# An expert mixture with a long convolution on one core: no GpSimd arithmetic in the head, tokens normalised inside the first expert, the first expert by halves

## The chip, the cores and the metric

The kernel runs on one core of a Trainium2 chip. TensorE (PE in the profile, with PEld for its weight loads), VectorE (DVE), ScalarE (ACT), GpSimd (POOL) and SyncE (SP) each take their own instructions in a fixed order and wait for each other by semaphores. DMA queues move data between HBM and the on-chip memory SBUF; matmul results land in PSUM. The metric is the device time of one execution in microseconds (us). "The span" is the stretch from the first to the last instruction in the profile.

## What is computed

Both branches read the same normalised tokens: a gated convolution (two depthwise convolutions over 2048 positions) and a mixture of 8 experts with 2 chosen for each token.

```python
def _A_ref(q, k, v, shift_k, ssm_k, ssm_D):          # B, S, D = 1, 2048, 512
    ...
    for t in range(ks):                                # ks = 4
        k_shift = k_shift + k_pad[:, t:t + S, :] * shift_k[:, ks - 1 - t][None, None, :]
    kv = k_shift * v
    ...                                                # y = long causal convolution of kv with ssm_k, by FFT
    y = y + kv * ssm_D[None, None, :]
    return q * y

def _B_ref(x, w_gate, w1, w2):                         # D, F, E = 512, 1792, 8
    ...
    logits = xf @ w_gate
    topk_idx = jnp.argsort(-logits, axis=-1)[:, :K]    # K = 2
    topk_val = jnp.take_along_axis(logits, topk_idx, axis=-1)
    gates = _softmax(topk_val, axis=-1)
    for e in range(E):
        mask = (topk_idx == e)
        w = (gates * mask).sum(-1, keepdims=True)
        h = _silu(xf @ w1[e]) @ w2[e]
        out = out + w * h
    ...

x = A_q
xn = _layernorm(x, axis=-1)
return x + _A_ref(xn, A_k, A_v, A_shift_k, A_ssm_k, A_ssm_D) + _B_ref(xn, B_w_gate, B_w1, B_w2)
```

## The kernel before

**Stages.** A head (`load_x`, `logits`, `routing`) finds for each token its two experts and for each expert the list of its tokens. Then eight experts run one after the other (`expert`), the fullest first, with 576 places for the first. The convolution's work is cut into small pieces which `fill` hands out between the matmuls of the experts. Three pieces of it, `conv_k` for the groups (0,3), (1,0) and (1,1), are recorded in `routing` instead, behind `prep(0)`; `conv_k` turns eight columns of the filter (`ptk`, L641), multiplies them by the transform's edge matrix (`ps`, L606) and stores them in `zk_d`.

**The token columns.** The 2048 tokens lie as 16 columns of 128 tokens by 512 numbers, in four tiles `x` of four columns, in a pool of their own. `bn_stats` gives mean and variance, `rstds` the scale `rstd` and the shift `nmr`. In `norm` GpSimd normalises twelve columns (L310) and ScalarE four (L307); `store_xn` writes them to `xn_d` in DRAM, from where the other experts gather their tokens.

**The first expert's tokens.** A one-hot table and matmuls (`ptab`) give the list of token numbers (`gix`). `gathers` then has GpSimd issue six indirect DMAs, each of which fetches 96 rows of the raw input into a block `xg`. The blocks are normalised by scales gathered through a second table matmul, three on ScalarE and three on VectorE (L847, L849). `turn` transposes them on TensorE into `ptm`, and since matmuls take numbers of reduced precision here, each operand is split in two: ScalarE rounds to `xh` ("high"), VectorE subtracts to `xl` ("low"). Weights are split the same way into `wh` and `wl`: `weights` loads 512 KB slices `wraw`, three buffers in turn.

**An expert.** `mm6` multiplies high by high, low by high and high by low. An expert has 14 hidden tiles (numbered 0 to 13 here): each is 24 matmuls into one of two PSUM tiles `ps`; ScalarE applies silu twice (`h` rounded, `ht` full), VectorE subtracts to the low part (L912). Two hidden tiles come from one weight slice. In the first expert `weights` has GpSimd make the low part `wl` of slices 1 to 5 (`lo_eng`), VectorE that of the others. Behind each hidden tile `fill` also does a step of `slots`, which makes the token lists of the other experts: VectorE writes a table (`tabA`, `tabB`, `tabR`), TensorE multiplies it (`ptab`, 128x216), VectorE adds the result to `tb`.

**What sets the order.** A scheduler sorts the recorded instructions of each engine with a time model of its own; a call `after(late, early, reason)` holds one instruction behind another without a wait. So the second half of the convolution's filter is held behind the gathers by a one-element GpSimd write:

```python
            if pair:
                self.after(nc.gpsimd.memset(t[:1, c, :1], 0.0), self.gather, "the first expert's tokens come first")
            nc.sync.dma_start(t[:, c, :], io["A_ssm_k"][dc * P:(dc + 1) * P, :])
```

Each engine then keeps that order: an instruction which waits holds back all behind it.

## Time and profile before

| what | value |
|---|---|
| time, median of 3 runs | 893.86 us (892.17 to 895.03) |
| the profiled execution's own time | 892.98 us |
| its span | 891.1 us |
| TensorE busy | 840.8 us (94%) |
| VectorE busy | 599.9 us (67%) |
| ScalarE busy | 501.0 us (56%) |
| GpSimd busy | 234.1 us (26%) |
| mean granted TensorE clock | 0.975 of full speed |

Rows of a timeline have the start in us from the span's start, the duration in us, the engine, the line, the operation, what it writes <- what it reads with shapes, and the count; in brackets stands how long the engine had been idle just before and who ended that. Rows of a table by stage have the stage, its length, then for each engine the busy us and the number of instructions, then the granted clock, the share of the DMA engines and GB/s.

### The profile page before, as it was taken

What the parts mean: (1) busy time and instruction counts of PE and PEld (TensorE: products, weight loads), DVE (VectorE), ACT (ScalarE), POOL (GpSimd) and SP (SyncE); (2) the same over time, 40 slices, a digit from 0 to 9 for tenths busy, and PEclk for the clock granted to TensorE, in tenths of its full rate; (3) what the DMA queues carried; (4) which work ended last, traced back from release to release, by engine and by line L of the source; (5) the groups of instructions that cost most, each with busy time, mean ns of one, the idle gap of its engine ahead of it and who ended that gap; (6) DMA issues with size and microseconds to landing.
All of it is one profiled execution on the core that took longest, in us unless ns stands there. A gap on an engine that the chain in (4) does not pass through costs nothing. (4 is left out here: it accounts for less than half of the span.)

```text
span 891.1 us, 13814 instructions
## 1 busy us (share of the span) xinstructions
PE 840.8 (94%) x5040; PEld 734.6 (82%) x5040; DVE 599.9 (67%) x841; ACT 501.0 (56%) x786; POOL 234.1 (26%) x202
## 2 busy tenths in 40 slices
PE   9807999999999998999999999999999989999996
PEld 7506899888999888999999988888888767777885
DVE  6893674679866765567766677658766649965421
ACT  4625542435533455666876668657875659654520
POOL 0090304046330440304310050103201123444222
PEclk9957999999999999999999999999999999999999
DMA  7595754999977676665965666557655499968972
GB/s 304 174 328 199 274 177 135 278 234 287 243 199 208 180 205 210 206 183 171 237 197 167 194 214 215 180 177 232 228 171 174 134 251 297 282 197 286 263 209 71
DMA packets 146497, 190.97 MB, mean 214 GB/s; under 512 B 12673, under 2 KB 106235, under 8 KB 144956
## 3 DMA queue, kind: packets, MB, share of 16 engines
q1 hardware_dynamic: 130348, 147.29, 54.4%
q0 software_dynamic: 16080, 42.78, 16.6%
q8 instruction: 41, 0.67, 0.3%
q14 instruction: 28, 0.23, 0.1%
HBM read 143.88 MB, written 50.63 MB: 218 GB/s over the span
## 5 line engine op out<-in xcount | busy, mean ns | idle before, releaser
L869 DVE TENSOR_TENSOR wl<-wraw,wh 128x1024 fp32r<-128x1024 f32 (+1 forms) x111 | 135.0, 1216 | 110.1 <-ACT wh L866 99.9
L866 ACT ACTIVATE wh<-wraw 128x1024 fp32r<-128x1024 f32 (+1 forms) x116 | 119.3, 1029 | 149.7 <-PE ps L884 109.9
L884 PE MATMUL ps<-xh,wh 128*128 128x512 f32 (+4 forms) x672 | 183.8, 328 | 5.6 <-ACT ht L911 2.9
L884 PE MATMUL ps<-xl,wh 128*128 128x512 f32 (+4 forms) x672 | 182.8, 326 | 0.0
L884 PE MATMUL ps<-xh,wl 128*128 128x512 f32 (+4 forms) x672 | 182.0, 325 | 0.0
L884 PE MATMUL ps<-h,wh 128*128 128x288 f32 (+3 forms) x896 | 154.3, 291 | 0.0
L884 PEld LDWEIGHTS ps<-h,wh 128*128 128x128 f32 x896 | 129.0, 189 | 5.6 <-issue 4.5
L884 PEld LDWEIGHTS ps<-xh,wh 128*128 128x128 f32 x672 | 113.7, 190 | 22.1 <-ACT ht L911 5.1
L884 PEld LDWEIGHTS ps<-xl,wh 128*128 128x128 f32 x672 | 114.2, 190 | 8.7
L884 PEld LDWEIGHTS ps<-xh,wl 128*128 128x128 f32 x672 | 113.8, 190 | 9.0
L912 DVE TENSOR_TENSOR h<-ht,h 128x512 fp32r<-128x512 f32 (+4 forms) x112 | 79.7, 717 | 44.3 <-ACT ht L911 44.1
L910 ACT ACTIVATE h<-ps 128x512 fp32r<-128x512 f32 (+4 forms) x112 | 67.8, 605 | 61.7 <-PE ps L884 58.1
L884 PE MATMUL ps<-h,wl 128*128 128x288 f32 (+3 forms) x448 | 95.5, 291 | 0.0
L957 PE MATMUL py<-wl,h 128*128 128x512 f32 x224 | 87.6, 391 | 0.0
L958 PE MATMUL py<-wh,h 128*128 128x512 f32 x224 | 87.5, 391 | 0.0
L956 PE MATMUL py<-wh,h 128*128 128x512 f32 x224 | 87.1, 392 | 0.0
L938 POOL DMA_INDIRECT acc_d<-acc,ids x36 | 54.0, 1499 | 120.7 <-DVE acc L936 114.0
L884 PEld LDWEIGHTS ps<-h,wl 128*128 128x128 f32 x448 | 71.7, 189 | 1.9 <-issue 1.5
L923 POOL DMA_INDIRECT acc<-acc_d,gix x36 | 46.8, 1300 | 99.1 <-PE ptx L828 64.3
L911 ACT ACTIVATE ht<-ps 128x512 f32<-128x512 f32 (+4 forms) x112 | 67.9, 609 | 0.0
L809 POOL DMA_INDIRECT xg<-xn_d,gix x34 | 41.4, 1218 | 82.2 <-PE ptx L828 40.6
L738 DVE TENSOR_TENSOR ka<-pu,ka 128x512 f32<-128x512 f32 x32 | 22.1, 691 | 50.5 <-ACT ka L733 43.2
(241 smaller groups left out, 1288.3 us busy)
## 6 DMA issues: line engine op xcount, KB each, us to landing
wraw<-in_B_w_dram SPq DMA_DIRECT2D x84, 512.0 KB, 4.6
wraw<-in_B_w_dram SPq DMA_DIRECT2D x32, 448.0 KB, 4.6
zk_d<-ev SPq DMA_DIRECT2D x16, 512.0 KB, 6.7
zv_d<-ev SPq DMA_DIRECT2D x16, 512.0 KB, 6.3
mid<-in_c_mid_dram POOLq DMA_DIRECT2D x16, 512.0 KB, 5.4
z<-zk_d SPq DMA_DIRECT2D x32, 256.0 KB, 3.0
z<-zv_d SPq DMA_DIRECT2D x32, 256.0 KB, 3.1
zi_d<-zo SPq DMA_DIRECT2D x32, 256.0 KB, 3.4
```

Source lines behind the costliest of these rows:

```text
L809: self.gather = nc.gpsimd.indirect_dma_start(out=t[:sb], out_offset=None, in_=self.xn_d[:, :] if r else self.io["A_q"].rearrange("o s d -> ...
L866: w = nc.scalar.activation(hi, raw, AF.Copy)
L869: t = (lo_eng or nc.vector).tensor_sub(lo, raw, hi)
L884: nc.tensor.matmul(ps[:, u, :n], w, x[:, u, :], start=first and w is wh and k == 0, stop=last and w is wl)
L910: nc.scalar.activation(h, ps[:, :nu, :n], AF.Silu)
L911: acts.append(nc.scalar.activation(t, ps[:, :nu, :n], AF.Silu))
L912: self.hid = nc.vector.tensor_sub(l, t, h)
L923: nc.gpsimd.indirect_dma_start(out=acc[:sb], out_offset=None, in_=sum_d[:, :], in_offset=bass.IndirectOffsetOnAxis(ap=self.gix[:sb, c0 + b ...
L938: st = nc.gpsimd.indirect_dma_start(out=sum_d[:, :], out_offset=bass.IndirectOffsetOnAxis(ap=self.ids[:sb, c0 + b:c0 + b + 1], axis=0), in ...
L956: nc.tensor.matmul(o, a, wh[:, f, :], start=ff == 0, stop=False)
L957: nc.tensor.matmul(o, a, wl[:, f, :], start=False, stop=False)
L958: nc.tensor.matmul(o, l, wh[:, f, :], start=False, stop=ff == FC - 1)
```

## The change

Four things change. **GpSimd computes nothing** any more in the head and the first expert: the low parts of weight slices 1 to 5 go to VectorE, the token columns to VectorE and ScalarE (eight each), and the one-element writes are gone, so that the filter's second half is loaded as soon as its queue allows. **The token columns** lie in eight tiles of two columns, in a pool `h2` under the names `h6` to `h13`: these are the places of the last eight hidden tiles. The first two tiles are normalised behind the first expert's tokens, tile i (2 to 7) behind hidden tile i-2, and each is stored at once; hidden tile 6+i is written into the place of token tile i. **The first expert begins by halves**: blocks 0 to 2 are normalised, transposed and split before blocks 3 to 5, and hidden tiles 0 and 1 are accumulated for the first half of the tokens, then for the second; VectorE normalises all six blocks. **The gates** are a tanh, from the table that also holds silu, in place of an exponential and a reciprocal. With this the order is written anew: the one-hot table in four parts, the gathers ahead of the three convolution groups and these ahead of the tokens, VectorE taking every second eviction of the last two groups, and the rest of the routing's arithmetic behind the last low part `xlo`.

```diff
     def load_x(...)
-            t = ep.tile([P, 4, D], F32, tag="x", name="x", bufs=4)
+            t = self.h2.tile([P, 2, D], F32, tag="h%d" % (FC - NI // 2 + i), name="x")
...
     def norm(self):
-                if j == 3:
-                    self.after(nc.scalar.activation(x[:, j, :], x[:, j, :], AF.Identity, bias=bi, scale=sc),
-                               self.parted, "the first expert comes first")
-                else:
-                    t = nc.gpsimd.tensor_scalar(x[:, j, :], x[:, j, :], sc, bi, op0=ALU.mult, op1=ALU.add)
-                    self.pool_norms.append(t)
...
+            v = nc.vector.tensor_scalar(self.x[2 * i], self.x[2 * i], sc, bi, op0=ALU.mult, op1=ALU.add)
+            sc, bi = self.rstd[:, 2 * i + 1:2 * i + 2], self.nmr[:, 2 * i + 1:2 * i + 2]
+            a = nc.scalar.activation(self.x[2 * i + 1], self.x[2 * i + 1], AF.Identity, bias=bi, scale=sc)
+            if i < 2:
+                self.after(v, self.xlo, "the first expert comes first")
+                self.after(a, self.xhi, "the first expert comes first")
+            else:
+                self.norms.append((v, a))
+            self.xs.append(nc.sync.dma_start(xnv[:, 2 * i:2 * i + 2, :], self.xt[i]))
...
     def routing(self, bp, sp, cp):
-        self.onehot(A0, f0, 2)
         self.columns(B0, q0)
...
+        self.rtid = self.onehot(A0, f0, 4, t)
...
+        t = nc.scalar.activation(self.warm, self.warm, AF.Silu)
+        self.after(t, self.rooted, "the square root comes first")
+        self.after(nc.scalar.activation(gt, gt, AF.Tanh, scale=0.5), t, "one table serves both")
...
+        self.gathers(0)
+        for pair, q8 in ((0, 3), (1, 0), (1, 1)):
+            for _ in self.conv_k(cp, pair, q8, pair == 1):
+                pass
         self.prep(0)
-        for pair, q8 in ((0, 3), (1, 0), (1, 1)):
-            for _ in self.conv_k(cp, pair, q8):
-                pass
-        self.store_xn()
...
-        self.after(V.tensor_mul(w8, ro, b1(rt["cap"])), self.indexed, "the routing comes first")
+        self.after(V.tensor_mul(w8, ro, b1(rt["cap"])), self.xlo, "the first expert comes first")
...
     def pairs(...)
-            for t, ev in zip(ps, evs):
-                nc.scalar.activation(ev[:, r, :], t, AF.Copy)
+            for k, (t, ev) in enumerate(zip(ps, evs)):
+                if shared and k:
+                    nc.vector.tensor_copy(ev[:, r, :], t)
+                else:
+                    nc.scalar.activation(ev[:, r, :], t, AF.Copy)
...
     def load_k(self, cp, pair):
-            if pair:
-                self.after(nc.gpsimd.memset(t[:1, c, :1], 0.0), self.gather, "the first expert's tokens come first")
...
     def prep(self, r):
-        for b in range(0 if r else NBLK[r]):
-            t, (sc, bi) = self.xg[b][:sb], (a[:sb, b:b + 1] for a in self.sc0)
-            if b % 2:
-                self.normed = nc.scalar.activation(t, t, AF.Identity, bias=bi, scale=sc)
-            else:
+        for u in range(2):
+            for b in range(3 * u, 3 * u + 3):
+                t, (sc, bi) = self.xg[b][:sb], (a[:sb, b:b + 1] for a in self.sc0)
                 nc.vector.tensor_scalar(t, t, sc, bi, op0=ALU.mult, op1=ALU.add)
+            self.turn(0, [u])
+            if u == 0:
+                self.half = self.xhi
+        self.norm()
...
     def weights(...)
-        t = (lo_eng or nc.vector).tensor_sub(lo, raw, hi)
-        if self.nw == 1:
+        t = nc.vector.tensor_sub(lo, raw, hi)
+        if self.nw < 3:
             self.after(t, self.scaled, "the first expert's tokens come first")
...
     def expert(self, hp, r, fill):
+            if r == 0 and s == 0:
+                ahead = [self.pmm.tile([P, 2, D], F32, tag="mm", name="ps") for _ in range(2)]
+                for u in range(nu):
+                    for f in range(2):
+                        for dc in range(DC):
+                            self.mm6(ahead[f], nu, n, wh[:, dc, f * P:(f + 1) * P], wl[:, dc, f * P:(f + 1) * P],
+                                     self.xh[dc], self.xl[dc], dc == 0, dc == DC - 1, u)
...
+                hl2 = (hp if ff < FC - NI // 2 else self.h2).tile([P, 2, nu, n], F32R, tag="h%d" % ff, name="h")
...
+                if self.norms:
+                    for late, early in zip(self.norms.pop(0), (self.hid, acts[-1])):
+                        self.after(late, early, "the first expert comes first")
...
```

How this moves the instructions stands below at three places; the rows are those of an engine's own order, with line, operation, what it writes <- what it reads and the shape. Numbers behind a name tell buffers apart.

**VectorE, around the first expert's tokens.** Names: `xg` a gathered block, `xl` the tokens' low part, `wl` a weight slice's low part, `ev` an evicted spectrum, `wk`, `o`, `ef`, `blk` arithmetic of the routing. Before:

```order
L474 TENSOR_TENSOR pos_488<-pos_488,iso_798 128x128
L511 TENSOR_SCALAR ef_849<-ef_849 1x32
L849 TENSOR_SCALAR xg_596<-xg_596,sc00_592,sc01_593 96x512
L479 TENSOR_TENSOR wk_814<-oh_448,pos_488 128x256
L512 CAST blk_85<-ef_849 1x32
L480 TENSOR_REDUCE o_805<-wk_814 128x32
```

Now:

```order
L845 TENSOR_SCALAR xg_619<-xg_619,sc00_607,sc01_608 96x512
L832 TENSOR_TENSOR xl_722<-ptx_726,xh_718 128x288
L832 TENSOR_TENSOR xl_723<-ptx_732,xh_719 128x288
L832 TENSOR_TENSOR xl_724<-ptx_738,xh_720 128x288
L832 TENSOR_TENSOR xl_725<-ptx_744,xh_721 128x288
L864 TENSOR_TENSOR wl_1063<-wraw_1060,wh_1062 128x1024
L845 TENSOR_SCALAR xg_621<-xg_621,sc00_607,sc01_608 96x512
L832 TENSOR_TENSOR xl_722<-ptx_753,xh_718 128x288
L832 TENSOR_TENSOR xl_723<-ptx_759,xh_719 128x288
L832 TENSOR_TENSOR xl_724<-ptx_765,xh_720 128x288
L832 TENSOR_TENSOR xl_725<-ptx_771,xh_721 128x288
L304 TENSOR_SCALAR x_106<-x_106,rstd_126,nmr_127 128x512
```

The routing's arithmetic stood between the blocks; all of it now stands behind the last low part and two token columns (`x`), and the third weight slice stands between the two halves. Ahead of these rows VectorE has, in this order: the first two weight slices, two evictions `ev`, the first three blocks, an eviction, a block, an eviction.

**VectorE, up to the first table of the other experts' lists.** Names: `h` a hidden tile's low part, `cc` the last of the routing's arithmetic, `tabA`, `tabB`, `tabR` the table. Before:

```order
L500 TENSOR_TENSOR cc_812<-cc_812,tq_811 128x32
L835 TENSOR_TENSOR xl_637<-ptm_638,xh_636 128x576
L835 TENSOR_TENSOR xl_648<-ptm_649,xh_647 128x576
L912 TENSOR_TENSOR h_908<-ht_907,h_908 128x576
L521 TENSOR_TENSOR tabA_913<-rc_116,f6_813 128x512
L527 TENSOR_TENSOR tabB_914<-rc_116,cc_812 128x288
```

Now:

```order
L496 TENSOR_TENSOR cc_836<-cc_836,tq_835 128x32
L912 TENSOR_TENSOR h_956<-ht_955,h_956 128x576
L304 TENSOR_SCALAR x_110<-x_110,rstd_126,nmr_127 128x512
L517 TENSOR_TENSOR tabA_961<-rc_123,f6_837 128x512
L526 TENSOR_TENSOR tabB_962<-rc_123,cc_836 128x288
L912 TENSOR_TENSOR h_967<-ht_966,h_967 128x576
L304 TENSOR_SCALAR x_112<-x_112,rstd_126,nmr_127 128x512
L534 TENSOR_TENSOR tabR_963<-tabB_962,tid2_870 128x4x72
```

The last of the arithmetic stood ahead of the tokens' last low parts; it now stands behind them, and a token column follows each hidden tile.

**TensorE, hidden tile 3 and the first table.** Names: `ps_998` and `ps_1021` are the PSUM tiles of hidden tile 3, `ptab` the table's product. Before:

```order
L884 MATMUL ps_998<-xh_636,wl_960 128x288 x2
L884 MATMUL ps_998<-xh_647,wh_959 128x288 x2
L884 MATMUL ps_998<-xl_648,wh_959 128x288 x2
L884 MATMUL ps_998<-xh_647,wl_960 128x288
L537 MATMUL ptab_948<-tabR_915,tabA_913 128x216 x4
```

Now:

```order
L876 MATMUL ps_1021<-xh_719,wh_982 128x288 x2
L876 MATMUL ps_1021<-xl_723,wh_982 128x288 x2
L876 MATMUL ps_1021<-xh_719,wl_983 128x288 x2
L536 MATMUL ptab_971<-tabR_963,tabA_961 128x216 x4
L876 MATMUL ps_1021<-xh_720,wh_982 128x288 x2
```

The table's product stood one matmul before the end of tile 3; it now stands in its middle, behind 12 of its 24 matmuls.

## What was predicted

> **What bounds the kernel now.** First the page: whose engine is the span. Then the busy times by stage, to see where that engine rests.
>
> ```profile
> span 891.1 us, 13814 instructions
> PE 840.8 (94%) x5040; PEld 734.6 (82%) x5040; DVE 599.9 (67%) x841; ACT 501.0 (56%) x786; POOL 234.1 (26%) x202
> ...
> 40.00:50.00 10.00, 3.02 (x34) 2.84 (x32) 6.39 (x42) 5.44 (x8) 6.04 (x6) 0.70 1.09 339
> 50.00:60.00 10.00, 0.00 (x0) 0.00 (x0) 10.00 (x6) 3.39 (x4) 10.00 (x11) 0.50 1.10 311
> 60.00:70.00 10.00, 2.00 (x9) 1.43 (x10) 9.83 (x24) 0.00 (x0) 7.04 (x10) 0.50 0.63 239
> ...
> 160.00:891.00 731.00, 714.25 (x4196) 624.02 (x4194) 495.46 (x586) 427.79 (x664) 190.06 (x153) 0.99 0.72 211
> ```
>
> TensorE (PE) works 94% of the span and 714 of the last 731 us, so the kernel is a queue of matmuls, and what an edit is worth is how much earlier that queue runs freely. It rests between 43 and 75 us: 5 of 30 us busy, at half the clock. So the next view is that stretch in order of time, engine by engine; each row has start, duration and engine.
>
> ```profile
> 39.98 1.52 PE L537 MATMUL ptab<-tabR,tabA 128*96 128x6 f32 x16
> 65.64 0.90 PE L828 MATMUL ptm<-ident,xg 96*128 96x96 f32 x4 [22.12 <-DVE xg L849]
> 75.00 0.85 PE L884 MATMUL ps<-xh,wh 128*128 128x288 f32 x2 [0.57 <-DVE xl L835]
> 83.86 1.99 PE L606 MATMUL ps<-kt,ev 64*128 64x512 f32 x8
> 91.51 0.63 PE L884 MATMUL ps<-xh,wh 128*128 128x288 f32 x2 [1.89 <-ACT ht L911]
> 95.53 0.42 PE L884 MATMUL ps<-xh,wh 128*128 128x288 f32 x2
> 95.79 0.43 PE L884 MATMUL ps<-xl,wh 128*128 128x288 f32 x2
> 99.97 0.30 PE L884 MATMUL ps<-xh,wh 128*128 128x288 f32 x1
> ...
> 51.13 14.02 DVE L511 TENSOR_SCALAR ef<-ef 1x32 f32<-1x32 f32 x1
> 65.06 0.53 DVE L849 TENSOR_SCALAR xg<-xg,sc,sc 96x512 f32<-96x512 f32 x1
> ...
> 52.23 4.63 POOL L869 TENSOR_TENSOR wl<-wraw,wh 128x1024 fp32r<-128x1024 f32 x2
> 56.86 9.72 POOL L310 TENSOR_SCALAR x<-x,rstd,nmr 128x512 f32<-128x512 f32 x12
> 66.55 0.48 POOL L628 TENSOR_TENSOR ks<-ks,dv 128x1 f32<-128x1 f32 x2
> ```
>
> TensorE waits 22.12 us for the first normalised token block, and that block waits behind one VectorE (DVE) instruction on 32 numbers that takes 14.02 us. GpSimd (POOL) computes without a pause from 52.23 to 66.6, so I read the 14 us as VectorE shut out by GpSimd. A second pair, forty microseconds later, says the same: a 0.46 us instruction (its neighbour at 99.51, below) takes 2.64 and ends as GpSimd's does.
>
> ```profile
> 93.57 2.56 POOL L869 TENSOR_TENSOR wl<-wraw,wh 128x1024 fp32r<-128x1024 f32 x1 [14.41 <-ACT wh L866]
> ...
> 93.80 2.64 DVE L535 TENSOR_TENSOR tabR<-tabB,tid 128x288 fp32r<-128x288 f32 x1
> ...
> 99.51 0.46 DVE L535 TENSOR_TENSOR tabR<-tabB,tid 128x288 fp32r<-128x288 f32 x1
> ```
>
> The Trainium skill, page "SBUF — State Buffer", section "Who interferes with whom", has it as a lock: a GpSimd instruction and certain VectorE ones share one port pair, and the later one stands still for the whole of the other. The trace agrees (14.02 and 2.64 us).
>
> After 75 us two costs remain: the last two convolution groups sit inside the first expert (83.86 on), and tile 2 of the expert starts cold at 91.51. Tile 4 starts at 99.97; from there on TensorE is full. **My mark is the start of tile 4**: before it everything is moved, behind it nothing but VectorE's load.
>
> **The change part by part.**
>
> *Step 1, the indices: +1.1 us.* The gathers now start when?
>
> ```profile
> 42.44 1.10 POOL L809 DMA_INDIRECT xg<-in_A_q_dram,gix  x1 [20.11 <-DVE tb L544]
> 48.75 2.72 POOL L809 DMA_INDIRECT xg<-in_A_q_dram,gix  x1 [0.30 <-issue]
> ...
> 44.11 1.28 ACT L449 ACT_TABLE_LOAD   x1
> ...
> DMA to landing us min/median/max: 6.0/6.8/8.8
> ```
>
> The one-hot table is cut in four and its matmuls follow piece by piece, which would save most of their 1.52 us. But on TensorE the products of group (0,3) now stand between the pieces, and they wait for ScalarE (ACT), whose table load of 1.28 us has moved ahead of those evictions. So the last piece ends near 43.0 in place of 41.5; VectorE's copy into SBUF drops out (0.2 us), the gate's logistic needs no exponential table and no wait. Bounds: 0 if the evictions lead anyway, +1.5 if all of the load shows. I take a start at 43.5.
>
> *Step 2, the landing: gather 3 at 52.8, gather 6 at 58.6.* The six issues come (48.75 - 42.44)/5 = 1.26 us apart. Gather 3: 43.5 + 2 × 1.26 + 6.8 (median). Gather 6: 43.5 + 5 × 1.26 + 8.8 (the longest, because the weight loads and spectrum stores are in flight now too; the DMA share was 1.09 to 1.10 before). Bounds for gather 6: 55.8 with 6.0, and 58.6 plus the extra issue time of rival 2. ssm_k's second half (2 MB) leaves this stretch for that of 20 to 30 us, whose DMA share is 0.02, and costs nothing there:
>
> ```profile
> 20.00:30.00 10.00, 8.49 (x52) 5.12 (x50) 9.33 (x29) 5.29 (x11) 0.19 (x1) 1.00 0.02 7
> ```
>
> *Step 3, convolution groups (1,0), (1,1): hidden, -7.6 us on the path.* They took TensorE from 83.86 to 91.51 with ScalarE's evictions. Now they stand between the gathers and the token transposes, in the 22 us hole. VectorE takes every second eviction. They pass if done by about 54, when half the tokens are there; without that cover each group costs about 4 us.
>
> *Step 4, tokens to VectorE's last low part: 61.4.* GpSimd computes nothing, so the 14.02 goes. VectorE does in this order (durations as start-to-start pitches of its rows): gather 3's block done 53.3; two evictions and two blocks to 55.7; four low parts of half width, 0.37 each (half of 0.75), 57.2; the third weight split, 1.13, 58.3; gather 6's block 59.1; transposes, ScalarE's high parts and four low parts, 61.4. The halves let TensorE do 12 matmuls of tile 0 in that time, no more. Bounds 58 (gather 6 at the median) to 66.
>
> *Step 5, VectorE's small arithmetic lands on the path: to 75.8.* Routing's second part, 56 small instructions that before lay beside the waiting, now stands behind the low parts, and the first slot table behind it.
>
> ```profile
> 45.73 0.24 DVE L456 TENSOR_TENSOR w<-ro,rt 128x64 f32<-128x64 f32 x1
> 49.07 1.20 DVE L869 TENSOR_TENSOR wl<-wraw,wh 128x1024 fp32r<-128x1024 f32 x1
> 50.20 0.27 DVE L472 TENSOR_TENSOR col<-col,cb 128x128 f32<-128x128 f32 x1
> 65.52 0.41 DVE L479 TENSOR_TENSOR wk<-oh,pos 128x256 f32<-128x256 f32 x1
> 72.31 0.75 DVE L835 TENSOR_TENSOR xl<-ptm,xh 128x576 fp32r<-128x576 f32 x1
> 72.98 0.18 DVE L500 TENSOR_TENSOR cc<-cc,tq 128x32 f32<-128x32 f32 x1
> 97.75 0.76 DVE L912 TENSOR_TENSOR h<-ht,h 128x576 fp32r<-128x576 f32 x1 [0.57 <-ACT ht L911]
> 98.42 0.68 DVE L521 TENSOR_TENSOR tabA<-rc,f 128x512 fp32r<-128x512 f32 x1
> 100.62 0.38 DVE L572 COPY tb<-ptab 128x216 f32<-128x216 f32 x1
> ```
>
> First part: 45.73 to 51.13 plus 0.16 is 5.56, less the split (50.20 - 49.07 = 1.13) and about 0.7 of six small ones that go or come earlier: 3.75. Second part: 65.52 to 73.10 is 7.58, less two token blocks (0.46 each) and two low parts (0.67 each): 5.3. With the first two token columns (0.46 each, as a block) 9.95: VectorE is at 71.35. Then, until the first slot table is written: two hidden tiles (98.42 - 97.75 = 0.67 each), two token columns, and table parts (100.62 - 98.42 = 2.2): 4.45. **Table ready at 75.8.**
>
> TensorE reaches that table's matmul in the middle of tile 3: behind the last low part 26 matmuls of tiles 0 and 1, 24 of tile 2, 12 of tile 3, at (95.79 - 95.53)/2 = 0.13 us: 62 × 0.134 = 8.3, so at 69.7. It waits 6.1 us, with tiles 3 to 13 queued behind. Before, VectorE had been idle there, and the table never waited:
>
> ```profile
> 91.49 0.76 DVE L912 TENSOR_TENSOR h<-ht,h 128x576 fp32r<-128x576 f32 x1 [15.58 <-ACT ht L911]
> ```
>
> The clock falls: rows 91.51 to 95.53 hold 18 matmuls in 4.02 us in place of 2.41, so 1.6 is lost. Tile 4 starts at 75.8 + 0.44 (table) + 12 × 0.134 + 1.6 = **79.45**, against 99.97: **-20.5 us**.
>
> *Step 6, later in the first expert: 0.* Five weight splits move from GpSimd (2.56 above) to VectorE (1.13), and of the sixteen token columns VectorE and ScalarE now take eight each. VectorE per two tiles: 2 × 0.67 + 2.2 + 0.36 + 1.13 + 2 × 0.46 = 5.95, TensorE 48 × 0.134 + 0.44 = 6.9. It keeps up by 0.9; if that is off by 1 us, three such pairs cost 3. Each of tiles 6 to 13 waits for its tokens' store: the column comes after tile i-2 and the place is wanted at tile i+6, eight tiles or 26 us later; the four stores before took 6.9 us to land:
>
> ```profile
> xn_d<-x SPq DMA_DIRECT2D x4, 1024.0 KB, 6.9
> ```
>
> Sum: 891.1 - 20.5 = 870.6 span. The profiled execution took 892.98 us (1.9 around the span), the median of three is 893.86, so the profile is 0.9 below that; my time is 870.6 + 1.9 = 872.5.
>
> **The rivals.**
>
> *1, no stall at the table.* If VectorE's small instructions run much faster than their rows, or TensorE is so slow and cold until then that it comes no earlier than the table, nothing waits: tile 4 at 61.4 + 74 × 0.134 + 0.44 = 71.8, gain 28.2, **864.8 us**. Against it: 14.4 us of VectorE stand against 8.3 of TensorE, in a fixed order.
>
> *2, gathers late.* The sixth gather's issue took 2.72 us, the five others about 0.92, and VectorE's 1.20 us split ran in it (49.07). Now two splits and two evictions run during gathers 4 to 6: (2.72 - 0.92) for two of them is 3.6, and the low parts end near 65: **876 us** (874 to 880). The same page of the Trainium skill, in "A bandwidth-pool intuition that's wrong", says GpSimd cannot write a gather's descriptors while VectorE holds the pair; by it the moved work, token blocks above all, hits the gathers. The 2.72 fits, and no run here yet shows which instruction does it.
>
> *3, the 14 us stay*, since GpSimd's gathers and not its arithmetic shut VectorE out: 872.5 + 14 = **886**. Against: the row ends with the arithmetic, 15 us after the last issue.
>
> *4, slower: the places.* The stores of pairs 2 to 7 stand on SyncE's queue behind a register load that waits for VectorE and behind weight loads. It decides when column, store and landing together exceed 26 us; six tiles then each wait, and one tile's time (3.2) each is 19 us, so a little over that is **897**. Against: 0.5 + 6.9 + the few us of queue.
>
> **How the numbers follow.** Forecast 0.54 (872), rival 1 0.13, rival 2 0.25, rival 3 0.04, rival 4 0.04. 864 to 880 holds the forecast with the last low part at 58 to 66 and a cold stall or not, and rivals 1 and 2. Under 0.3% (2.7 us) this kernel's measurement cannot tell a change from none. Faster 0.95, same 0.02, slower 0.03 (rival 4, split).
>
> **What would show it.** Step 1: first gather near 43.5. Step 2: VectorE's last token block near 58.6 and no 14 us instruction. Step 3: no spectrum products after 56. Step 5: TensorE idle about 6 us before the first 128x216 table matmul, released by VectorE, and a half clock behind it; without that idle time rival 1 is right. Rival 2: issues above 2 us. Step 6: no wait of the activation on a store, TensorE full from tile 4 on. The forecast is wrong if the gathers land outside 55 to 61, or if TensorE stalls again at a later table.

## The result

The changed kernel takes 872.7 us (median of four runs, 872.59 to 874.25) against 894.44 us before (four runs, 892.17 to 895.2): the ratio is 0.9765, 95% interval 0.9743 to 0.9787. A second set of runs, in a later sitting, gave 872.66 us (six runs, 870.28 to 875.4) and 0.9786 (0.9757 to 0.9814). Forecast were 872.5 us and a range of 864 to 880.

The page of the changed kernel and its busy times by stage (stage, length, busy us and instructions of TensorE, its weight loads, VectorE, ScalarE and GpSimd, then the granted clock, the DMA share and GB/s):

```profile
span 872.5 us, 13843 instructions
PE 843.4 (97%) x5040; PEld 735.1 (84%) x5040; DVE 597.2 (68%) x864; ACT 499.3 (57%) x786; POOL 209.8 (24%) x183
...
50.00:60.00 10.00, 7.75 (x32) 4.88 (x33) 6.88 (x13) 5.58 (x11) 0.44 (x1) 0.57 1.03 323
...
70.00:80.00 10.00, 5.29 (x41) 5.06 (x39) 9.69 (x44) 4.73 (x7) 0.60 (x1) 0.96 0.92 226
80.00:90.00 10.00, 9.82 (x55) 9.82 (x56) 7.64 (x14) 4.51 (x7) 0.00 (x0) 0.70 0.87 297
```

The 22 us hole is gone: TensorE works 7.75 us between 50 and 60, where it did nothing, though at a clock of 0.57. A smaller hole has come between 70 and 80 (5.29 us busy), where VectorE is at 9.69 of 10, and a low clock (0.70) behind it. The timeline of the changed kernel shows what stands there, first TensorE, then VectorE, ScalarE and GpSimd:

```profile
54.15 3.85 PE L605 MATMUL ps<-kt,ev 64*128 64x512 f32 x8
57.93 1.31 PE L829 MATMUL ptx<-ident,xg 96*128 96x96 f32 x9
67.16 0.40 PE L876 MATMUL ps<-xh,wh 128*128 128x288 f32 x1 [1.15 <-DVE ov L456]
80.18 1.19 PE L536 MATMUL ptab<-tabR,tabA 128*128 128x216 f32 x4 [4.89 <-DVE tabR L534]
81.17 0.71 PE L876 MATMUL ps<-xh,wh 128*128 128x288 f32 x2
84.08 0.68 PE L876 MATMUL ps<-xh,wh 128*128 128x288 f32 x2
86.00 0.44 PE L876 MATMUL ps<-xl,wh 128*128 128x288 f32 x2
...
59.15 1.61 DVE L832 TENSOR_TENSOR xl<-ptx,xh 128x288 fp32r<-128x288 f32 x4
61.25 1.22 DVE L864 TENSOR_TENSOR wl<-wraw,wh 128x1024 fp32r<-128x1024 f32 x1 [0.49 <-ACT wh L861]
62.40 0.54 DVE L845 TENSOR_SCALAR xg<-xg,sc,sc 96x512 f32<-96x512 f32 x1
63.77 1.55 DVE L832 TENSOR_TENSOR xl<-ptx,xh 128x288 fp32r<-128x288 f32 x4 [0.84 <-ACT xh L831]
65.24 0.99 DVE L304 TENSOR_SCALAR x<-x,rstd,nmr 128x512 f32<-128x512 f32 x2
70.17 0.16 DVE L507 TENSOR_SCALAR ef<-ef 1x32 f32<-1x32 f32 x1
75.60 0.19 DVE L496 TENSOR_TENSOR cc<-cc,tq 128x32 f32<-128x32 f32 x1
79.67 0.46 DVE L534 TENSOR_TENSOR tabR<-tabB,gl 128x288 fp32r<-128x288 f32 x1
...
50.66 1.06 ACT L861 ACTIVATE wh<-wraw 128x1024 fp32r<-128x1024 f32 x1 [3.11 <-DMA wraw<-in_B_w_dram]
...
43.20 1.12 POOL L810 DMA_INDIRECT xg<-in_A_q_dram,gix  x1 [3.74 <-DVE ids L544]
49.52 0.92 POOL L810 DMA_INDIRECT xg<-in_A_q_dram,gix  x1 [0.30 <-issue]
```

The instruction on 32 numbers takes 0.16 us (70.17), no longer 14.02. TensorE waits 4.89 us for the first slot table (80.18), and the 20 matmuls behind it, 81.17 to 86.00, take 4.83 us where 2.65 is the full pace (20 times the 0.13 us of the rows behind them). Hidden tile 4, the prediction's mark, begins at 84.08: 15.9 us earlier than before, where 20.5 were forecast. The time came out as forecast all the same, so something behind the mark must have covered the miss ahead of it. The experiments look for both.

### The profile page after: what moved, and what is told of

Read it like the earlier page. It is cut to its first block, busy times and chain, and to the rows that moved or that the text cites. A ratio compares the mean times of both kernels' runs of the same rounds, so it can differ in the third digit from the quotient of the medians.

```text
span 872.5 us, 13843 instructions
## 1 busy us (share of the span) xinstructions
PE 843.4 (97%) x5040; PEld 735.1 (84%) x5040; DVE 597.2 (68%) x864; ACT 499.3 (57%) x786; POOL 209.8 (24%) x183
## 5 line engine op out<-in xcount | busy, mean ns | idle before, releaser
L864 DVE TENSOR_TENSOR wl<-wraw,wh 128x1024 fp32r<-128x1024 f32 (+1 forms) x116 | 140.2, 1209 | 116.0 <-ACT wh L861 105.7
L876 PE MATMUL ps<-xh,wh 128*128 128x512 f32 (+4 forms) x672 | 185.8, 329 | 3.0 <-DVE ov L456 1.2
L876 PE MATMUL ps<-xl,wh 128*128 128x512 f32 (+4 forms) x672 | 184.8, 327 | 0.1
```

The source lines that it names most:

```text
L864: t = nc.vector.tensor_sub(lo, raw, hi)
L876: nc.tensor.matmul(ps[:, u, :n], w, x[:, u, :], start=first and w is wh and k == 0, stop=last and w is wl)
```

## The experiments

**Does the stall at the table cost what it seems to?** First `slots` is begun two hidden tiles later.

```diff
             def fill(r):
-                next(slots, None)
                 self.points += 1
+                if self.points > 2:
+                    next(slots, None)
```

> The steps of the other experts' token lists begin two hidden tiles later, nothing else changes. Theory (TensorE stands at the first table because VectorE's small arithmetic has come behind the tokens): TensorE reaches the table 49 matmuls later, near 81.6, VectorE has written it near 82.5, so of the 4.89 us wait about 0.9 stays and the half clock behind it goes (20 matmuls from 81.17 to 86.00 in 4.83 us instead of 2.65, and the table's own 0.99 instead of 0.44). Gain 4.0 + 2.2 + 0.55 = 6.7 us: 866. Rival (VectorE is behind for the whole first expert, the wait only moves to a later table): gain under 2 us, 871 to 873, with a wait of 4 us or more at another table.

Measured: 868.33 us (868.06 to 872.98), ratio to the kernel before 0.9733 (0.9691 to 0.9775). TensorE's timeline with this edit:

```profile
75.33 0.42 PE L876 MATMUL ps<-xh,wh 128*128 128x288 f32 x2
81.05 0.70 PE L536 MATMUL ptab<-tabR,tabA 128*128 128x216 f32 x4 [0.90 <-DVE tabR L534]
```

The wait is 0.90, as worked out, the table takes 0.70 and not 1.19, the clock stays up, no later table waits, and tile 4 begins at 75.33, tile 6 8.4 us earlier than in the changed kernel. The wait is a matter of place: the same arithmetic, two tiles further behind, is almost hidden. Not all of the 8.4 us is this edit's: the last low part ends at 63.81 here and at 65.32 in the changed kernel, over code that is the same up to there. The hold near the end (tested below) leaves the head as it is, and in its profile the last low part ends at 63.83, the table waits 4.88 us and tile 4 begins at 82.57; against that profile tile 4 comes 7.2 us earlier and tile 6 6.9, of which a table that is still to come takes back 0.4. That is near the 6.7 worked out, and 4.4 of it reach the end.

**Is the late weight slice the cause of the late tokens?** The high part of the second slice, for which ScalarE waits 3.11 us above, is held behind the first half of the tokens.

```diff
-        if self.nw == 3:
+        if self.nw in (2, 3):
             self.after(w, self.half, "the first expert's tokens come first")
```

> The high part of the second weight slice is held behind the first half of the tokens on ScalarE. Theory (ScalarE waited 3.11 us for that slice and held back the evictions of the convolution groups, TensorE's transposes of the filter and with them VectorE's token blocks): the groups' products end near 55 instead of 58, the last low part near 62 instead of 65.3, everything behind moves with it: gain 3.3 us, 869.4. Rival (the tokens' landing or VectorE's own work holds the low parts, the wait at ScalarE was covered): the last low part stays within 0.5 us of 65.3 and the time at 872 to 873.

Measured: 872.69 us (871.73 to 874.78), 0.9762 (0.973 to 0.9794): no gain. The last low part begins at 62.59 (63.77 in the changed kernel), but in the kernel above, whose code is the same up to there, it began at 62.26 without this edit. The 3.11 us is the wait of one execution (1.26 in a second profile of the changed kernel), and my theory of it falls.

**What does the arithmetic ahead of the table cost?** The routing's second part is held behind the scales only, no longer behind the last low part.

```diff
-            self.after(t, self.xlo, "the first expert comes first")
+            self.after(t, self.scaled, "the first expert comes first")
...
-        self.after(V.tensor_mul(w8, ro, b1(rt["cap"])), self.xlo, "the first expert comes first")
+        self.after(V.tensor_mul(w8, ro, b1(rt["cap"])), self.scaled, "the first expert comes first")
```

> The routing's second part of arithmetic is no longer held behind the last low part, only behind the scales. Theory (it is what stands ahead of the first table, and its instruction at L456 keeps one of two PSUM tiles, so that hidden tile 1 cannot begin by its first half): VectorE does most of it in its idle time between 46 and 58, from the last low part to the table are left 1.0 + 3.7 + 4.4 us instead of 14.9; TensorE does 24 and not 12 matmuls ahead of the second half, its 1.15 us wait released by L456 is gone; the table is ready near 75.3 instead of 80.1. Gain 4.8 us, 868, up to 2 more if the clock no longer falls. Rival (the small instructions between blocks and low parts delay the tokens by as much): last low part 2 us later or more, gain under 2.5 us, 870.5 to 873.

Measured: 869.22 us (863.67 to 870.66), 0.9714 (0.9664 to 0.9763). VectorE's last low part, then TensorE's waits:

```profile
67.91 0.45 DVE L832 TENSOR_TENSOR xl<-ptx,xh 128x288 fp32r<-128x288 f32 x1
...
70.78 0.53 PE L876 MATMUL ps<-xh,wh 128*128 128x288 f32 x2 [1.02 <-ACT ht L911]
77.33 0.70 PE L536 MATMUL ptab<-tabR,tabA 128*128 128x216 f32 x4 [1.51 <-DVE tabR L534]
```

Both are right in part. The low parts come 3 us later than in the changed kernel's first profile, as the rival says, but the table 2.9 us earlier (77.33), the wait is 1.51 and the clock stays up; tile 4 begins at 79.47. The wait at L456 is gone, so it was the PSUM tile: the routing's counts `pw` lie in one of the two buffers of `pmm` and are read last by that instruction, which the change had moved behind the tokens. A wait of 1.02 us for the silu of tiles 0 and 1, which now end together, has taken its place.

**Do the three add up?**

> The three edits together. Theory (three separate delays of one chain): last low part near 62, 24 matmuls ahead of it, no wait at the first table, no half clock behind; hidden tile 4 begins at 62 + 72 x 0.1315 = 71.5 instead of 84.1, gain 12.6 us: 860. Rival (VectorE's whole load up to tile 6 is the bound, so the edits share one gain): 865 to 867, with waits for VectorE in tiles 2 to 6 of 4 us or more together.

Measured: 867.69 us (five runs, 863.73 to 868.93), 0.9711 (0.9679 to 0.9742). Neither forecast holds. The last low part ends at 66.34, not 62, tile 4 begins at 75.6, not 71.5, and the waits of the rival are absent: no table waits. And yet the time is no better than with the slot lists alone (868.33). The profiled run was the fastest of the five, 863.73, and lacked a wait that the changed kernel's profile has near 710 us. Here the two, ScalarE and TensorE of the changed kernel, then ScalarE and TensorE of the three edits:

```profile
709.85 1.06 ACT L583 ACTIVATE hi<-zb 128x1024 fp32r<-128x1024 f32 x1 [5.95 <-DMA zb<-zi_d]
710.96 1.22 PE L782 MATMUL psb<-hi,ei 128*128 128x512 f32 x2 [2.75 <-ACT hi L583]
713.24 0.63 PE L876 MATMUL ps<-xh,wh 128*128 128x512 f32 x1
```

```profile
698.19 1.06 ACT L583 ACTIVATE hi<-zb 128x1024 fp32r<-128x1024 f32 x1 [3.60 <-DMA zb<-zi_d]
699.30 0.74 PE L782 MATMUL psb<-hi,ei 128*128 128x512 f32 x2 [0.39 <-ACT hi L583]
```

The convolution's last stage reads back rows `zi_d` that the stage before has just written. Where they land late, TensorE waits 2.75 us and then runs at a lower clock (0.50 from 713.0 to 717.5: ten matmuls of 512 columns take 4.25 us from 713.24 on, where the ten behind them take 2.3). In ten profiles, all taken here of the changed kernel and of experiments without the next edit, the wait was 0.39 to 4.32 us.

**Is it this wait that eats the gains?** The split of those rows is held behind hidden tile 8 of expert 6, so that TensorE comes to them 48 matmuls later.

```diff
-            nc.scalar.activation(hi, src, AF.Copy)
+            self.split = nc.scalar.activation(hi, src, AF.Copy)
...
+        if i == 0:
+            self.first = self.split
...
                 acts.append(nc.scalar.activation(t, ps[:, :nu, :n], AF.Silu))
+                if r == E - 2 and ff == 8:
+                    self.after(self.first, acts[-1], "the last group's rows land first")
```

> The changed kernel with one hold at its end: the split of the convolution's first output rows (hi of zb) is held behind hidden tile 8 of the last expert but one, so that TensorE comes to them 48 matmuls, 10.9 us, later. Theory (TensorE waits there 2.4 to 4.3 us for rows that are read back from DRAM, and runs some 6 us at half the clock behind it; of two runs of the three edits together, one without that wait took 863.73, the median of all 867.69): gain 4 us, 868.7, no wait above 0.6 us between 690 and 740. Rival (the convolution's last units set the end, and what is not waited for here is waited for later): 871.5 to 874.

> The three edits and the hold at the end. Theory (the gain of the three at hidden tile 6, 9.3 us, is lost in most runs to the wait near 700 us): 863.5, 9 us below the changed kernel. Rival (the gain is lost for another reason): 866.5 to 868.5, like the three edits alone.

Measured, in one sitting: 869.08 us (867.13 to 870.67), ratio 0.974 (0.9696 to 0.9784), with the hold alone, and 866.27 us (862.93 to 866.91), 0.9705 (0.9657 to 0.9752), with all four edits. The wait at the read-back rows is gone from both profiles, but another has come behind it, where I had forecast none above 0.6 (changed kernel with the hold; with all four edits it is 1.49):

```profile
721.67 0.51 PE L878 MATMUL ps<-xh,wh 128*128 128x512 f32 x1 [2.29 <-ACT ht L913]
```

The hold alone brought 3.6 us against the changed kernel, near the 4 forecast, though in another sitting and with overlapping intervals. On top of the three edits, whose runs were of an earlier sitting, it brought 1.4 us, not 4, so in that pair it is unclear. A pair in one sitting, below, says more.

**What was hiding the convolution groups worth?** In the changed kernel they go back behind the tokens.

```diff
         self.gathers(0)
+        self.prep(0)
         for pair, q8 in ((0, 3), (1, 0), (1, 1)):
             for _ in self.conv_k(cp, pair, q8, pair == 1):
                 pass
-        self.prep(0)
```

> The changed kernel with the three convolution groups recorded behind the tokens again, as before the change. Theory (step 3 of the prediction: hidden in the hole they are worth 7.6 us): hidden tile 4 of the first expert begins 7 us later, 880. Rival (the stall at the first table takes that gain back, since VectorE's arithmetic is late either way; and without the groups the tokens come 3 us earlier): the groups fill the 4.89 us stall, which is gone, tile 4 begins within 2 us of 84.1, 871 to 875.

Measured: 875.35 us (874.58 to 876.38), 0.9815 (0.9772 to 0.9858). Its VectorE rows of the last token block and the last low part, then TensorE's last products, the first slot table and two late waits:

```profile
54.58 0.54 DVE L845 TENSOR_SCALAR xg<-xg,sc,sc 96x512 f32<-96x512 f32 x1 [0.52 <-DMA xg<-in_A_q_dram,gix]
60.52 0.46 DVE L832 TENSOR_TENSOR xl<-ptx,xh 128x288 fp32r<-128x288 f32 x1 [0.79 <-ACT xh L831]
...
79.14 1.99 PE L605 MATMUL ps<-kt,ev 64*128 64x512 f32 x8
85.81 0.60 PE L536 MATMUL ptab<-tabR,tabA 128*128 128x216 f32 x4
...
711.83 1.22 PE L782 MATMUL psb<-hi,ei 128*128 128x512 f32 x2 [3.45 <-ACT hi L583]
791.19 0.47 PE L876 MATMUL ps<-xh,wh 128*128 128x512 f32 x1 [1.78 <-DVE acc L939]
```

The rival is nearer in both: the table does not wait, and tile 4 begins at 81.69, 2.4 us ahead of 84.08. Without the groups the gathers start at 41.04 instead of 43.20, the last token block is normalised at 54.58, as soon as its gather has landed, and the last low part ends at 60.98, against 63.83 to 65.94 in three profiles with the changed kernel's head. So the groups were not free in the hole: they delay the tokens by 3 to 5 us. The version is still some 2.7 us slower than the changed kernel at the end, though at tile 4 it is 0.9 to 2.7 us ahead of those three; what it loses lies behind, among it the waits at 711.83 and 791.19, of which both profiles of the changed kernel lack the second. Why they are longer here is open, and so is how much of the 2.7 us belongs to the groups.

**Was it GpSimd's arithmetic that shut VectorE out?** The kernel before, with GpSimd's token columns held behind the first expert's last low part.

```diff
                     t = nc.gpsimd.tensor_scalar(x[:, j, :], x[:, j, :], sc, bi, op0=ALU.mult, op1=ALU.add)
+                    self.after(t, self.split, "the first expert comes first")
                     self.pool_norms.append(t)
...
-                nc.vector.tensor_sub(l, pm[:, :, :cap // nu], h)
+                self.split = nc.vector.tensor_sub(l, pm[:, :, :cap // nu], h)
```

> The kernel before, with one edit: GpSimd's twelve token columns are held behind the first expert's last low part instead of starting at 56.9. GpSimd's arithmetic beside the routing is then 4.63 us of weight splits instead of 14.4 us. Theory (VectorE's instruction of 14.02 us is shut out by GpSimd's arithmetic): that row shrinks to 5 us or less, the first token transposes begin near 57.5 instead of 65.6, and the time falls by 6 to 8 us, to 886 to 888. Rival (the gathers shut VectorE out, or the tokens land only then): the row stays above 10 us, the time within 2 us of the kernel before.

Measured: 881.14 us (879.65 to 884.58), 0.9887 (0.9836 to 0.9937), 10.7 us below the kernel before in the same sitting, with no overlap of their runs, and 3 to 5 more than forecast: half of what the whole change brings, from one hold. Where the further microseconds come from was not looked for. VectorE, GpSimd and TensorE of this kernel:

```profile
50.68 5.77 DVE L512 TENSOR_SCALAR ef<-ef 1x32 f32<-1x32 f32 x1
62.29 0.48 DVE L490 TENSOR_TENSOR f<-f,tq 128x32 f32<-128x32 f32 x1
62.70 0.18 DVE L490 TENSOR_TENSOR r<-r,f 128x32 f32<-128x32 f32 x1
...
51.78 4.63 POOL L870 TENSOR_TENSOR wl<-wraw,wh 128x1024 fp32r<-128x1024 f32 x2
61.95 9.15 POOL L310 TENSOR_SCALAR x<-x,rstd,nmr 128x512 f32<-128x512 f32 x12
...
56.96 0.90 PE L829 MATMUL ptm<-ident,xg 96*128 96x96 f32 x4 [13.53 <-DVE xg L850]
```

The long row ends at 56.45, GpSimd's two splits at 56.41, and the transposes begin at 56.96 instead of 65.64. With the twelve columns out of the way, the same small instruction is held 5.77 us by two splits instead of 14.02 us by splits and columns. The gathers are the same in both kernels (the sixth is issued from 48.67 to 51.02, and the row outlasts it by 5.4 us), so they are not the cause; this answers the prediction's third rival.

**Would GpSimd be of use again, now that the columns are gone?** The low parts of slices 1 to 5 go back to it.

```diff
-        t = nc.vector.tensor_sub(lo, raw, hi)
+        t = (lo_eng or nc.vector).tensor_sub(lo, raw, hi)
...
             wh, wl = self.weights(w1v[:, :, s * 256:(s + 1) * 256], [P, DC, 256],
+                                  nc.gpsimd if r == 0 and 0 < s < 6 else None,
```

> The changed kernel with the low parts of weight slices 1 to 5 given back to GpSimd, as before the change; the token columns stay with VectorE and ScalarE. Step 6 of the prediction (VectorE keeps up by 0.9 us per two tiles, the move costs nothing): no gain from giving them back, 872 to 874; where a split of 2.4 to 2.6 us meets a VectorE instruction, that one is as long, but behind the tokens it delays nothing. Rival (VectorE's load sets the first expert): 1.2 us less work ahead of the last low part and 1.2 less ahead of the second table, gain 1.2 us or more, 871.5 or less. Second rival (GpSimd's arithmetic shuts VectorE out among the token blocks too): 2 us or more lost, 875.

Measured: 875.7 us (874.46 to 877.12), 0.9817 (0.9791 to 0.9843), 3 us slower than the changed kernel in the same sitting (872.66), though the intervals overlap. GpSimd, VectorE and TensorE:

```profile
71.91 2.41 POOL L864 TENSOR_TENSOR wl<-wraw,wh 128x1024 fp32r<-128x1024 f32 x1 [1.91 <-ACT wh L861]
...
72.01 2.36 DVE L486 TENSOR_TENSOR f<-f,i 128x32 f32<-128x32 f32 x1
...
80.66 1.19 PE L536 MATMUL ptab<-tabR,tabA 128*128 128x216 f32 x4 [7.04 <-DVE tabR L534]
```

The time is the second rival's, the place is not. Among the token blocks a split (51.26 to 53.65) does hold VectorE, and two blocks from 52.61 on take 1.77 us instead of 0.99, but VectorE then waits 1.82 us before its next row (56.20), so nothing is lost there; the split from 60.70 to 63.07 holds no row. Behind the tokens one split meets one instruction of the small arithmetic, whose neighbours take 0.19 us; it takes 2.36, and the wait at the table grows from 4.88 to 7.04. Against the changed kernel's own two profiles the table is no later (80.66; 80.18 and 80.80), because here the last low part ends at 63.64; against the profile with the hold, whose low part ends at 63.83, it is 2.0 us later (78.67). So the small arithmetic is what sets the table, and the GpSimd split that met it is paid nearly in full. How much of the 3 us at the end is this split is not shown: tile 4 begins at 84.56, 0.2 to 2.0 us behind those profiles, and the waits at 711.61 (3.16 us) and 791.63 (1.75) follow.

**The changed kernel once more, and the two causes taken together.** The third kernel of this sitting begins `slots` three tiles later and moves only what frees the PSUM tile (L452, L453, L456) ahead of the tokens; the fourth adds the hold near 700 us.

```diff
-        self.after(V.tensor_mul(w8, ro, b1(rt["cap"])), self.xlo, "the first expert comes first")
+        self.after(V.tensor_mul(w8, ro, b1(rt["cap"])), self.scaled, "the scales come first")
         V.tensor_reduce(cap, w8, axis=AX.X, op=ALU.add)
-        V.tensor_mul(w8, ro, b1(rt["col0"]))
+        V.tensor_sub(ov, pn[:, :E], cap)
+        self.after(V.tensor_mul(w8, ro, b1(rt["col0"])), self.xlo, "the first expert comes first")
         V.tensor_reduce(cb, w8, axis=AX.X, op=ALU.add)
-        V.tensor_sub(ov, pn[:, :E], cap)
...
-                next(slots, None)
                 self.points += 1
+                if self.points > 3:
+                    next(slots, None)
```

> The changed kernel once more, on the chip of the next three, to see how far its own rows move from one profiled execution to the next. If the places of the waits belong to the program: 871 to 874, 4.5 to 5 us at the first table again, 2.4 to 4.3 near 710. If they are one execution's accident: the wait at the table differs by over 1.5 us.

> The changed kernel with the token lists begun three hidden tiles later, and with three small instructions (L452, L453, L456) ahead of the tokens, so that the PSUM tile they read is free. Theory (the wait at the table and the PSUM tile are two separate costs): 24 matmuls ahead of the second half, 1.7 us earlier than with the first alone (868.3), no wait at a table above 0.3 us: 865.7, tile 6 near 80.7. Rival (the tokens' landing, not TensorE's order, sets the end of tile 1): 867.5 to 869.

> The same, and the hold of the convolution's first output rows near 700 us. Theory (that wait costs 2 to 4 us in most executions of any of these kernels): 863, below every kernel so far. Rival (what is not waited for there is waited for later): within 1 us of the version without the hold.

Measured: 872.66 us (870.28 to 875.4) for the changed kernel; 869.9 us (868.15 to 873.48), ratio to before 0.9761 (0.9734 to 0.9787), without the hold; 864.85 us (863.89 to 866.46), 0.9703 (0.9677 to 0.9729), with it. TensorE of the changed kernel's second profile, then of the version without the hold:

```profile
80.80 1.19 PE L536 MATMUL ptab<-tabR,tabA 128*128 128x216 f32 x4 [4.88 <-DVE tabR L534]
84.38 0.42 PE L876 MATMUL ps<-xh,wh 128*128 128x288 f32 x2
...
710.25 0.73 PE L782 MATMUL psb<-hi,ei 128*128 128x512 f32 x2 [0.70 <-ACT hi L583]
```

```profile
83.17 0.60 PE L536 MATMUL ptab<-tabR,tabA 128*128 128x216 f32 x4
...
704.83 1.22 PE L782 MATMUL psb<-hi,ei 128*128 128x512 f32 x2 [2.87 <-ACT hi L583]
```

The stall at the table is the program's: 4.88 and 4.89 us, and 4.88 with the hold. Tile 4 is less fixed: 84.38, 84.08 and, with the hold, 82.57. The wait near 710 is not: 0.70 here, 2.75 in the first profile. Without the hold, tile 6 begins at 80.78 (80.7 expected), yet the time is 2.8 us below the changed kernel and not 7; the profile has the wait of 2.87 us. With the hold it is 5.0 us less again, and the runs of the two do not overlap. At tile 6 the head gains 9.4 to 11.0 us over the three profiles above, of which two tables still to come take back 0.9. Of that some 9 us, then, 2.8 reach the end without the hold and 7.8 with it: the wait, with the low clock behind it, takes about half. The last version is faster than both kernels: 7.8 us (0.9%) below the changed one, in one sitting and with no overlap of their runs.

## Why the prediction was right, and where it was not

The sum came out right although the mark missed by 4.6 us: the part behind it, which I had set to no change, came out shorter, and the executions compared made up the rest.

**Step 4 failed, by 3.9 us, because of step 3.** The last low part was to end at 61.4 and ended at 65.32; the last token block was at 62.40 instead of 58.6. The landing (step 2) was not late in this profile: the gathers took 6.4 to 8.1 us from issue to landing, so the sixth, issued at 49.52, had landed by 57.6. The failed step is the word "hidden" in **step 3**: I counted the groups as free if they were done by 54, and they ended at 58.0 (54.15 + 3.85; the same eight products take 1.99 us at full clock), with four of their evictions ahead of the last blocks on VectorE. TensorE's first transposes of tokens stand behind the groups and begin at 57.93, so the first half's low parts end at 60.76 (59.15 + 1.61) instead of 57.2. That is 3.5 of the 3.9 us; the third split and the last block follow as in my order, only later.

That the kernel without the groups comes to 60.98, close to 61.4, is a coincidence: its gathers start 2.2 us earlier, its last block is normalised 4 us ahead of my 58.6, and from there the low parts take 6.4 us where I had 2.8. The size of the miss moves, too: the last low part ends at 65.94 in the second profile of the changed kernel and at 63.83 in the profile with the hold, whose head is the same, so step 4 was off by 2.4 to 4.5 us. The saving of 7.6 us in step 3 was mis-sized: with the groups put back the time rises by 2.7, since the tokens come sooner and the groups fill the stall at the table.

**Step 5 was right in mechanism and nearly in size.** From the last low part to the end of the small arithmetic 10.5 us (65.24 to 75.71, where the next row starts; forecast 9.95), table parts 4.4 (4.45), ready at 80.1 instead of 75.8, which is step 4's error carried on. TensorE came at 75.3, since it too was late, so the wait is 4.89, not 6.1. Ahead of the mark the half clock cost 1.3 us on matmuls (12 in 2.91) and 0.55 on the table, in the second profile 1.0 and 0.55 (ten matmuls in 2.33 us), where I had 1.6. What I overlooked is that the moved arithmetic keeps a PSUM tile: 1.15 us at 67.16.

**The cover.** Behind tile 4 the changed kernel takes 788.4 us (872.5 - 84.08) and 787.2 in its second profile, the kernel before 791.1. I had set this to no change. In fourteen profiles, one for each kernel and two of the changed one, it ranges from 785.9 to 792.8, mainly by the waits near 325, 710 and 790 us, so the 2.7 to 3.9 us can't be put down to the change. Forecast mark -20.5 and rest 0 are -20.5; measured -15.9 and -2.7 are -18.6 between two profiles, of which that of before was 1.5 us below its median and that of the changed kernel 1.5 above; hence -21.7 between medians. My 872.5 was counted from that low execution of before without a correction. The hit within 0.2 us is partly luck; the range was not.

**What is not divided up.** The token columns were tested alone in the kernel before (10.7 us), the groups and the splits by taking them back (2.7 and 3.0, with overlapping intervals). The halves, the tanh, the one-hot table in quarters and the filter's earlier load were not run alone, so their shares of the 21.7 us are not shown.

**Step 1** held in the profile (43.20, forecast 43.5), and not in general: see below. **Step 6** held: no activation waits for a store, and TensorE has no wait above 0.3 us from 86 to 288 us.

**Rivals.** 1 (no stall) is wrong, twice 4.9 us. 2 (gathers shut out) is wrong in the first profile, where all six issues take 0.92 to 1.12 us although a VectorE split (47.09 to 48.33) runs beside the fourth, and right in part in the second. There the same program's gathers start 2.8 us later, two splits (50.17 to 52.52) and an eviction run beside the fifth issue, and GpSimd has this row:

```profile
51.12 2.19 POOL L810 DMA_INDIRECT xg<-in_A_q_dram,gix  x1 [0.30 <-issue]
```

So its sign, an issue above 2 us, came in one of two profiles: the fifth block then waits 1.09 us for its landing, and the last low part ends at 65.94, near the 65 that it names. But the issue loses 1.3 us and not 3.6, and that sitting's median of 872.66 us is not its 876. Five other profiles with the late start have 1.06 to 1.35 us for the fifth issue. Which instruction beside an issue lengthens it stays open; a split alone is not enough. 3 is answered by the columns' experiment. 4 is wrong by the absence of any wait on a store (its 897 is also 5.5 us above the 872.5 + 19 that it works out).

## What to carry to other kernels

When work is moved into a hole, price it against whatever the hole was waiting for, not against the hole's length: it runs on the same engines that prepare the end of the wait. When a stall lies between two moved chains, ask which small instructions one engine must still do ahead of the waiting table, and begin the table later before making it faster. And before adding up gains at the front, look in two profiles for waits at the back that are longer in one than in the other: those can take a part of any gain.

## What the hardware showed that I had not expected

**TensorE's clock in the head has two cases.** The changed kernel interleaves products and pieces of the index table. From the same program, the first profile: the busy times of one stage, and two rows of TensorE's timeline there.

```profile
39.40:42.00 2.60, 2.60 (x14) 1.07 (x14) 2.53 (x21) 1.56 (x5) 0.05 (x1) 1.00 1.15 346
...
37.89 0.71 PE L641 MATMUL ptk<-ident,ks 128*128 128x128 f32 x4 [1.27 <-ACT ev L610]
39.32 1.13 PE L605 MATMUL ps<-kt,ev 64*128 64x512 f32 x4 [0.45 <-ACT kt L642]
```

The second profile, the same two views (the row ahead is as above, 0.12 us later):

```profile
39.40:42.00 2.60, 2.56 (x8) 1.06 (x8) 2.53 (x20) 1.03 (x3) 0.18 (x1) 0.54 1.14 344
...
39.44 1.97 PE L605 MATMUL ps<-kt,ev 64*128 64x512 f32 x4 [0.46 <-ACT kt L642]
```

Behind the same short waits the granted clock is 1.00 or 0.54, the same four products take 1.13 or 1.97 us, and the first gather starts at 43.20 or 46.01. Of twelve profiles with the changed head five start at 42.95 to 43.61 and six at 45.43 to 46.09; the one without the groups starts at 41.04. Tile 4 does not follow it: 84.08 with the early start, 84.38 and, in the profile with the hold, 82.57 with the late one. The Trainium skill, page "TensorE: Matmul & The Clock Gate", section "What's actually happening", says that the clock is set by the activity in windows which run freely, so that where a window falls decides when it changes; two outcomes from one program agree with that. That it takes a whole idle window of some 3.4 us to lower the clock, as the section has it, does not fit, if idle means without work: the longest wait ahead was 1.27 us, and from 36.0 to 39.4 us TensorE was busy for 1.7 of 3.4 us in both profiles. Whether part of that work counts as none is not shown here. A wait of 1.15 us at 67.16, between long runs of matmuls, left the clock up.

**Not all GpSimd arithmetic shuts VectorE out alike.** A split holds a small VectorE instruction for its whole length (2.36 of 2.41 us, and 5.77 us until the end of two), on 32 numbers as on 4096. But beside the twelve columns that run from 61.95 to 71.1 in the kernel before with one edit, VectorE's instructions on two tensors went on, and only two took longer (0.48 at 62.29 instead of 0.18 as at 62.70, and 0.60 at 63.79). The Trainium skill, page "SBUF — State Buffer", section "Who interferes with whom", has a VectorE instruction with two inputs in SBUF contend with a GpSimd instruction that reads SBUF; the split agrees in full, the columns only at those two rows. Nor is the 14.02 us one instruction's length, as the prediction reads it: it outlasts two splits (4.63 us) and most of the columns. Why the columns let these pass while the one-input instruction of the kernel before stood for 14.02 us, to 1.4 us before the last column's end, is open.
